# Attention with squared relu and a mixture of experts on one core: blank list entries written in order, first expert tiles gathered sooner, V's parts ahead of the scores

## The chip, the core and the metric

The kernel runs on one core of a Trainium2 chip. The metric is device microseconds of one execution; a kernel's time is the median of its runs. The engines are TensorE (PE, with its weight loads PEld), VectorE (DVE), ScalarE (ACT), GpSimd (POOL) and SyncE (SP), which only issues copies. Lines such as L143 are lines of the kernel before.

## The reference

Eight batches of 2496 tokens go through attention with squared relu instead of a softmax, and the result is gated by u. Every token then goes to the one expert of eight that its logits choose.

```python
scores = (1.0 / S) * np.matmul(z, z.transpose(0, 2, 1))     # z: 8 x 2496 x 64
x = u * np.matmul(np.maximum(scores, 0.0) ** 2, v)          # u, v: 8 x 2496 x 256

logits = x @ w_gate                                         # 19968 tokens, 8 experts
expert_idx = np.argmax(logits, axis=1)
probs = softmax(logits)                                     # gate_w: the chosen one's
for e in range(E):
    xe = x[expert_idx == e]
    out[expert_idx == e] = gate_w * (np.maximum(xe @ w1[e], 0.0) @ w2[e])   # 256 x 1024, 1024 x 256
```

## The kernel before

**Numbers in two parts.** Products are made in float32r with each operand split into a high part, a cast (`hi`, `xh`, `vt[:, 0]`), and a low part, the rest (`lo`, `xl`, `vt[:, 1]`). The cast is mostly ACT's work, the subtraction DVE's or POOL's.

**Attention.** Queries are taken in five chunks (`c`, 512 wide, the last 448), keys in ten pairs of 128 (`kp`), so there are 8 x 5 x 10 = 400 steps (`steps`, the last is `LAST` = 399, `NKP` = 10). In a step, `weighted` (L325 to L328) multiplies V's pair by the scores of this step, 12 matmuls, and `scores` runs three steps ahead (`LA` = 3): four matmuls (L299, L300), a relu out of PSUM (L301), a square (L302) and a cast (L304) on ACT, the low part (L306) on DVE. Scores are symmetric: a block above the diagonal is transposed on DVE (`turn`, L267), written to DRAM (L270) and reloaded for a later chunk (`bring`, L277), where it needs only a cast (L291) and a subtraction (L292). At the end of a chunk `gate_x` multiplies the sum by u on DVE (L350). z, u and V are loaded by SP (L121, L151, L138), V into a ring of four raw blocks; `split_v` casts a V pair on ACT (L143) and subtracts on DVE or, from the third pair of the first batch, on POOL (L145).

**Routing.** For each chunk `turn_rows` writes x's rows to DRAM (`xrows`, L370) and `route` computes the expert of each token, its gate and its place; `place` scatters a 64-byte entry (gate, token number) per token to `lst` (L445, POOL). Each expert has a region of `lst`, big enough for all tokens. Places that no token takes must hold a blank entry (token number past the end), so `blank` (L233) writes blank entries over the places that a batch may reach, half a batch per call: 104 x 8 x 192 values, 624 KB. The calls for batch 0 and the tails of the regions stand in `constants`, on POOL; those for batch b + 1 stand at the sixth and ninth step of chunk 1 of batch b, on SP.

**Experts.** After batch 6 a first list (`A`) of tiles of 512 tokens is made from the regions that are already full, so that six tiles can run while the rest is still routed; after batch 7 a second list (`F`). For a tile, POOL loads its entries (`load_e`, L659), gathers its token rows (`load_x`, L670) and the expert's weights (`load_w`, L644, two halves of 1 MB each); `turn_x` transposes the rows on DVE (L700), writes them to DRAM (L703) and reloads them (L705); `split_x` casts them (L715, ACT) and subtracts (L716, DVE); `up` and `down` multiply (L733, L754, L756); `finish` scatters the rows to the output (L767). The work ahead of the first tile is put at steps counted from the last one (`loads`).

**What sets the order.** A scheduler orders the instructions of each engine's queue by priority and by its own simulated time, so an instruction with nothing to wait for may be moved well ahead of its place in the program. Within `pinned`, an instruction is kept behind the last one of its engine that stands ahead in the program. `declare_no_dep` tells the scheduler that two accesses of the same tensor don't touch the same places, so neither waits for the other. Each engine, SP too, issues in order.

Of the kernel before, what the change touches and what calls it, by code (L numbers as in the profile page):

```python
# [19 lines left out]
P = 128  # L20
# [3 lines left out]
E = 8  # L24
F = 1024
QC = 512
ENT, PAD = 16, 12
BIG, SMALL = 512, 256
# [20 lines left out]
def fused_kernel(ctx: ExitStack, tc: tile.TileContext, zt, ut, v, wg, wcat, out):  # L49
    nc = tc.nc  # L50
    B, _, SP = zt.shape
    S = SP - KQ
    NK = SP // P
    NKP = NK // 2
    NTOK = B * S
    chunks = [(q, min(QC, S - q)) for q in range(0, S, QC)]
    NC_ = len(chunks)
# [148 lines left out]
    def constants():  # L206
        nc.vector.memset(wg2.bitcast(F32), 0.0)
        nc.vector.tensor_copy(wg2[:, :, 0:E], wg_sb)
        nc.vector.tensor_tensor(wg2[:, :, E:2 * E], wg_sb, wg2[:, :, 0:E].bitcast(F32), op=ALU.subtract)
        for ti, tf in iotas:  # L210
            nc.vector.tensor_copy(tf, ti)
        nc.vector.tensor_copy(base, base0)

        nc.vector.memset(padrow, 0.0)
        nc.gpsimd.dma_start(xrows[NTOK:NTOK + 1, :], padrow)
        nc.gpsimd.memset(pad, 0.0)
        nc.gpsimd.iota(pad.bitcast(I32)[:, 1:PAD * ENT:ENT], pattern=[[0, PAD]], base=NTOK, channel_multiplier=0)
        blank(0, 0, nc.gpsimd)
        blank(0, 1, nc.gpsimd)
        w = BIG * ENT // P  # L220
        nc.gpsimd.dma_start(regions[:, NTOK * ENT:].rearrange("e (p k) -> p e k", k=w),
                            pad[:, 0:w].unsqueeze(1).broadcast_to([P, E, w]))
        nc.gpsimd.dma_start(lst[NROW * SMALL:].rearrange("(p r) k -> p (r k)", p=P), pad[:, 0:w])

    regions = lst[0:E * CAP].rearrange("(e c) k -> e (c k)", e=E)
    blanks, scatters = [], []

    def blank(b, h, eng=None):

        w, n = PAD * ENT, S // PAD // 2  # L230
        assert n * PAD * 2 == S and n <= P
        at = (b * S + h * S // 2) * ENT
        i = (eng or nc.sync).dma_start(regions[:, at:at + n * w].rearrange("e (p k) -> p e k", k=w),  # L233
                                       pad[0:n].unsqueeze(1).broadcast_to([n, E, w]))
        for _, o in scatters:
            tc.declare_no_dep(i.ins, o.ins, reason="places of another batch")
        blanks.append((b, i))
# [153 lines left out]
    def route(t0, n, ns, lw, gw):  # L391
# [28 lines left out]
        def place():  # L420
# [22 lines left out]
            for j in range(ns):  # L443
                m = min(P, n - j * P)
                i = nc.gpsimd.indirect_dma_start(  # L445
                    out=lst, out_offset=bass.IndirectOffsetOnAxis(ap=posi[:m, j:j + 1], axis=0),
                    in_=gw[:m, j, :], in_offset=None)
                for _, o in scatters:
                    tc.declare_no_dep(i.ins, o.ins, reason="places are distinct")
                for of, o in blanks:  # L450
                    if of > t0 // S:
                        tc.declare_no_dep(i.ins, o.ins, reason="places of another batch")
                scatters.append((t0 // S, i))

        return [choose, exps, place]
# [194 lines left out]
    def load_e(i):  # L650
        which, t, k = order[i]
        en = ents[i] = sb.tile([P, BS, ENT], F32, name="ent", bufs=6)
        to = en.rearrange("p s w -> p (s w)")
        eidx = lists[which]["eidx"]
        parts = [(by4, t, 0, BS)] if k == BS else [(by2, t, 0, 2)]
        if k == 3:
            parts.append((lst, eidx.shape[1] - N3 + t - 2 * ND - NB, 2, 3))
        for src, at, a, z in parts:
            nc.gpsimd.indirect_dma_start(out=to[:, a * ENT:z * ENT], out_offset=None, in_=src,  # L659
                                         in_offset=bass.IndirectOffsetOnAxis(ap=eidx[:, at:at + 1], axis=0))  # L660

    def token(i, s):
        return bass.IndirectOffsetOnAxis(ap=ents[i].bitcast(I32)[:, s, 1:2], axis=0)
# [154 lines left out]
    def at(s, work):  # L818
        todo.setdefault(s, []).append(work)

    for b in range(B):
        for c in range(NC_):
            s0 = (b * NC_ + c) * NKP
            at(s0 + 2, lambda b=b, c=c: fetch_u(b, c))
            if c == 1 and b + 1 < B:
                for h in range(2):
                    at(s0 + 5 + 3 * h, lambda b=b, h=h: blank(b + 1, h))
            if b == 0:
                continue
            f, z = {0: (-NKP * 4 + 1, 4), 1: (-NKP * 4 + 1, 4), 2: (-NKP * 4 + 1, 4), 3: (-NKP * 5 + 4, 7), 4: (-NKP * 4, 3)}[c]  # L830
# [2 lines left out]
        for kp in range(NKP):  # L833
            if b:
# [8 lines left out]
    ready[2] = scores(*steps[2])  # L843
    bg.append(constants)
    later = []
    loads = {NKP + 4: [lambda: load_e(0)],
             NKP + 3: [lambda: load_e(1)],
             NKP + 2: [lambda: load_x(0)],
             NKP + 1: [lambda: load_w(0, 0)],
             NKP - 1: [lambda: load_w(0, 1)],  # L850
             NKP - 3: [lambda: load_w(1, 0)],
             NKP - 4: [lambda: load_x(1)],
             NKP - 5: [lambda: turn_x(0), lambda: load_e(2)],
             1: [lambda: load_x(2), lambda: load_e(3)],
             0: [lambda: turn_x(1)]}
    for q in range(LP + 1):
# [1 line left out]
    for s, (b, c, kp) in enumerate(steps):  # L858
# [7 lines left out]
                fetch_v(0, kp + 2)  # L866
        for key in plan.get(s, []):
            bring(*key)
        if s + LA <= LAST:
            ready[s + LA] = scores(*steps[s + LA])  # L870
        if s < NKP:
            if kp + 1 < NKP:
                pinned(lambda: split_v(0, kp + 1))
            if kp % 2 == 0 and kp // 2 + 2 < NC_:
                pinned(lambda: split_z(0, kp // 2 + 2))
        if s == LAST - 1:
            pinned(lambda: split_x(0))
        weighted(b, c, kp, j == 0, j == NKP - 1, *ready.pop(s), accs[b, c])
# [118 lines left out]
```

## Time and profile before

| | us |
|---|---|
| median of 3 runs | 2303.61 |
| lowest, highest | 2300.22, 2307.38 |
| the profiled execution | 2306.15 |
| its span, first to last instruction | 2304.4 |
| PE busy in the span | 2233.8 (97%) |
| DVE, ACT, POOL busy | 1653.1 (72%), 1368.1 (59%), 673.9 (29%) |
| mean granted clock of PE, 1 is full speed | 0.989 |

The profile is of one execution. Attention takes some 1364 us of the span, the experts the rest. Busy PE is time in which matmuls run; the ends of matmuls are modelled, and at half clock the same matmul counts as longer. The idle time in front of an instruction is put down to what released it. Full clock is 2.4 GHz, half is 1.2.

### The profile page before, as it was taken

Reading aid. Unit: us, or ns where it says so; the run is one execution under the profiler, and the core shown is the slowest. Engines: PE = TensorE matmul, PEld = TensorE weight load, DVE = VectorE, ACT = ScalarE, POOL = GpSimd, SP = SyncE. Lnnn points to the kernel's source line nnn. Section 1 sums busy time; section 2 is a strip of 40 time slices with the busy share of each in tenths; the row PEclk is TensorE's granted clock in tenths of the full one; section 3 lists DMA queues with packets and bytes.
Section 4 is the critical chain, followed back from the end, with each engine's and each line's share of the span. In section 5 each row is a group of like instructions: output and inputs, shape, how many; then the busy total and the mean of one; then the engine's idle time right before and its main releaser. Section 6 shows DMA issues by size and latency. Waiting matters only on the chain. (4 is left out here: it accounts for less than half of the span.)

```text
span 2304.4 us, 31091 instructions
## 1 busy us (share of the span) xinstructions
PE 2233.8 (97%) x10864; PEld 1864.5 (81%) x10864; DVE 1653.1 (72%) x2798; ACT 1368.1 (59%) x1818; POOL 673.9 (29%) x724
## 2 busy tenths in 40 slices
PE   5999999999999999999999989999999999999997
PEld 3788788788888888887887878888888888888886
DVE  5687887887887888878878767566566675666653
ACT  4667757857768658667667643454454454554543
POOL 2210020120120120210220344545445555545521
PEclk8999999999999999999999999999999999999999
DMA  8865774775666756657657674555465556556520
GB/s 263 248 183 146 220 191 138 221 178 172 202 162 181 222 141 195 194 142 230 178 129 215 188 225 140 193 166 183 136 200 187 185 186 193 180 164 223 180 87 22
DMA packets 247180, 414.28 MB, mean 180 GB/s; under 512 B 105539, under 2 KB 146056, under 8 KB 227558
## 3 DMA queue, kind: packets, MB, share of 16 engines
q1 hardware_dynamic: 214006, 291.08, 44.1%
q0 software_dynamic: 33008, 121.12, 16.5%
q8 instruction: 87, 1.43, 0.3%
q14 instruction: 79, 0.65, 0.1%
HBM read 254.55 MB, written 158.07 MB: 179 GB/s over the span
## 5 line engine op out<-in xcount | busy, mean ns | idle before, releaser
L325 PE MATMUL acc<-thi,t 128*128 128x512 f32 (+1 forms) x1200 | 453.8, 389 | 23.8 <-ACT t L143 21.2
L328 PE MATMUL acc<-thi,t 128*128 128x512 f32 (+1 forms) x1200 | 462.3, 388 | 0.9 <-POOL t L145 0.5
L445 POOL DMA_INDIRECT lst<-gw,posi x160 | 172.6, 1078 | 963.9 <-DVE posi L442 468.0
L327 PE MATMUL acc<-tlo,t 128*128 128x512 f32 (+1 forms) x1144 | 444.4, 389 | 0.9 <-DVE tlo L306 0.5
L737 ACT ACTIVATE t<-ph 128x512 fp32r<-128x512 f32 (+1 forms) x328 | 192.5, 588 | 342.2 <-PE ph L733 262.0
L733 PE MATMUL ph<-thi,t 128*128 128x512 f32 (+2 forms) x1248 | 377.8, 362 | 14.7 <-ACT thi L715 9.2
L738 DVE SCALAR_TENSOR_TENSOR t<-ph,t 128x512 fp32r<-128x512 f32 (+1 forms) x328 | 220.5, 674 | 229.8 <-ACT t L737 190.6
L754 PE MATMUL y<-t,t 128*128 128x512 f32 x1062 | 379.3, 397 | 1.7 <-DVE tf L765 1.4
L301 ACT ACTIVATE tf<-ps_s 128x1024 f32<-128x1024 f32 (+1 forms) x240 | 242.2, 1017 | 231.5 <-PE ps_s L300 224.5
L756 PE MATMUL y<-t,t 128*128 128x256 f32 x1062 | 290.0, 281 | 2.3 <-DVE t L738 2.3
L325 PEld LDWEIGHTS acc<-thi,t 128*128 128x128 f32 x1200 | 226.3, 189 | 71.3 <-ACT t L143 24.0
L733 PEld LDWEIGHTS ph<-thi,t 128*128 128x128 f32 x1248 | 226.4, 190 | 52.5 <-ACT thi L715 9.3
L328 PEld LDWEIGHTS acc<-thi,t 128*128 128x128 f32 x1200 | 226.8, 189 | 43.9 <-POOL t L145 1.9
L302 ACT ACTIVATE tf<-tf 128x1024 f32<-128x1024 f32 (+1 forms) x240 | 250.4, 1053 | 4.6
L327 PEld LDWEIGHTS acc<-tlo,t 128*128 128x128 f32 x1144 | 216.7, 189 | 42.9 <-DVE tlo L306 3.5
L306 DVE TENSOR_TENSOR tlo<-tf,thi 128x1024 fp32r<-128x1024 f32 (+1 forms) x168 | 203.6, 1215 | 62.0 <-ACT thi L304 59.4
L754 PEld LDWEIGHTS y<-t,t 128*128 128x128 f32 x1062 | 198.0, 188 | 44.7 <-DVE tf L765 1.8
L267 DVE STREAM_TRANSPOSE s<-tf 128x1024 f32<-128x1024 f32 x160 | 197.5, 1235 | 47.1 <-ACT tf L302 42.7
L733 PE MATMUL ph<-tlo,t 128*128 128x512 f32 (+2 forms) x624 | 225.7, 362 | 2.2 <-issue 1.5
L767 POOL DMA_INDIRECT out_dram<-tf,ent x160 | 165.6, 1035 | 184.5 <-DVE tf L765 125.0
L756 PEld LDWEIGHTS y<-t,t 128*128 128x128 f32 x1062 | 200.5, 189 | 14.8 <-DVE t L738 3.7
L670 POOL DMA_INDIRECT rows<-xrows,ent x160 | 164.5, 1028 | 107.5 <-DMA ent<-lst,lfeidx 64.9
(238 smaller groups left out, 3962.7 us busy)
## 6 DMA issues: line engine op xcount, KB each, us to landing
scr<-s SPq DMA_DIRECT2D x80, 1024.0 KB
s<-scr SPq DMA_DIRECT2D x320, 256.0 KB
vr<-in_v_dram SPq DMA_DIRECT2D x80, 256.0 KB
u<-in_ut_dram SPq DMA_DIRECT2D x32, 512.0 KB
xrows<-th SPq DMA_DIRECT2D x128, 128.0 KB
far<-th SPq DMA_DIRECT2D x31, 512.0 KB
th<-far SPq DMA_DIRECT2D x124, 128.0 KB
zr<-in_zt_dram SPq DMA_DIRECT2D x36, 256.0 KB
```

Of the source, the lines that this page charges most:

```text
L267: nc.vector.transpose(out=to, in_=a.rearrange("p i (t s k) -> p i t s k", t=4, s=G))
L301: nc.scalar.activation(a[:, :, :n], ps[:, :, :n], AF.Relu)
L302: nc.scalar.activation(a[:, :, :n], a[:, :, :n], AF.Square)
L306: nc.vector.tensor_tensor(lo[:, :, :n], a[:, :, :n], hi[:, :, :n].bitcast(F32), op=ALU.subtract)
L325: nc.tensor.matmul(acc[d][:, :n], lhsT=vh, rhs=hi[:, i, :n], start=first and i == 0, stop=False)
L327: nc.tensor.matmul(acc[d][:, :n], lhsT=vh, rhs=lo[:, i, :n], start=False, stop=False)
L328: nc.tensor.matmul(acc[d][:, :n], lhsT=vl, rhs=hi[:, i, :n], start=False, stop=last and i == 1)
L733: nc.tensor.matmul(o, lhsT=w1[:, part, dd, fs], rhs=xx[:, dd, :n], start=p == 0, stop=p == 5)
L737: nc.scalar.activation(hh[:, :m], ph[:, :m], AF.Relu)
L738: nc.vector.scalar_tensor_tensor(hl[:, :m], ph[:, :m], 0.0, hh[:, :m].bitcast(F32), op0=ALU.max, op1=ALU.subtract)
L754: nc.tensor.matmul(y, lhsT=hh[:, cs], rhs=w2[:, f % 2].rearrange("p i d -> p (i d)"), start=f == 0, stop=False)
L756: nc.tensor.matmul(y[:, 0:D], lhsT=hl[:, cs], rhs=w2[:, f % 2, 0, :], start=False, stop=f == NF - 1)
```

## The change

It has three parts. First, the blanks: those of batch 0 and the tails move from POOL to SP and from `constants` to steps 6, 7 and 8, and every blank is now pinned to its place. Second, the first expert tiles: entries, rows and the transpose of the first tiles stand at earlier steps, the weights at the same ones, and the entry loads of list `A` and the scatters of the last batch are declared to have no dependence on each other. Third, in the first chunk of the first batch `split_v` for the next step stands ahead of `scores` in a step instead of behind.

```diff
-        blank(0, 0, nc.gpsimd)
-        blank(0, 1, nc.gpsimd)
+    def tails():
         w = BIG * ENT // P
-        nc.gpsimd.dma_start(regions[:, NTOK * ENT:].rearrange("e (p k) -> p e k", k=w),
-                            pad[:, 0:w].unsqueeze(1).broadcast_to([P, E, w]))
-        nc.gpsimd.dma_start(lst[NROW * SMALL:].rearrange("(p r) k -> p (r k)", p=P), pad[:, 0:w])
+        nc.sync.dma_start(regions[:, NTOK * ENT:].rearrange("e (p k) -> p e k", k=w),
+                          pad[:, 0:w].unsqueeze(1).broadcast_to([P, E, w]))
+        nc.sync.dma_start(lst[NROW * SMALL:].rearrange("(p r) k -> p (r k)", p=P), pad[:, 0:w])
...
-        i = (eng or nc.sync).dma_start(regions[:, at:at + n * w].rearrange("e (p k) -> p e k", k=w),
+        i = nc.sync.dma_start(regions[:, at:at + n * w].rearrange("e (p k) -> p e k", k=w),
...
+                for o in firsts:
+                    tc.declare_no_dep(i.ins, o.ins, reason="places of an earlier batch")
                 scatters.append((t0 // S, i))
...
-            nc.gpsimd.indirect_dma_start(out=to[:, a * ENT:z * ENT], out_offset=None, in_=src,
-                                         in_offset=bass.IndirectOffsetOnAxis(ap=eidx[:, at:at + 1], axis=0))
+            d = nc.gpsimd.indirect_dma_start(out=to[:, a * ENT:z * ENT], out_offset=None, in_=src,
+                                             in_offset=bass.IndirectOffsetOnAxis(ap=eidx[:, at:at + 1], axis=0))
+            if which == "A":
+                firsts.append(d)
+                for of, o in scatters:
+                    if of == B - 1:
+                        tc.declare_no_dep(d.ins, o.ins, reason="places of a later batch")
...
+    for h in range(2):
+        at(6 + h, lambda h=h: pinned(lambda: blank(0, h)))
+    at(8, lambda: pinned(tails))
...
-                    at(s0 + 5 + 3 * h, lambda b=b, h=h: blank(b + 1, h))
+                    at(s0 + 5 + 3 * h, lambda b=b, h=h: pinned(lambda: blank(b + 1, h)))
...
-    loads = {NKP + 4: [lambda: load_e(0)],
-             NKP + 3: [lambda: load_e(1)],
-             NKP + 2: [lambda: load_x(0)],
+    loads = {2 * NKP - 2: [lambda: load_e(0)],
+             2 * NKP - 3: [lambda: load_e(1)],
+             NKP + 4: [lambda: load_x(0)],
+             NKP + 3: [lambda: load_e(2)],
              NKP + 1: [lambda: load_w(0, 0)],
+             NKP: [lambda: load_x(1)],
              NKP - 1: [lambda: load_w(0, 1)],
              NKP - 3: [lambda: load_w(1, 0)],
-             NKP - 4: [lambda: load_x(1)],
-             NKP - 5: [lambda: turn_x(0), lambda: load_e(2)],
+             NKP - 2: [lambda: turn_x(0)],
              1: [lambda: load_x(2), lambda: load_e(3)],
              0: [lambda: turn_x(1)]}
...
+        if s < NKP and kp + 1 < NKP:
+            pinned(lambda: split_v(0, kp + 1))
         if s + LA <= LAST:
             ready[s + LA] = scores(*steps[s + LA])
-        if s < NKP:
-            if kp + 1 < NKP:
-                pinned(lambda: split_v(0, kp + 1))
-            if kp % 2 == 0 and kp // 2 + 2 < NC_:
-                pinned(lambda: split_z(0, kp // 2 + 2))
+        if s < NKP and kp % 2 == 0 and kp // 2 + 2 < NC_:
+            pinned(lambda: split_z(0, kp // 2 + 2))
```

## Rows read from the trace of the kernel before

**Rows 1.** The page, parts 1 and 2: PE's busy time, granted clock by slice.

```profile
PE 2233.8 (97%) x10864; PEld 1864.5 (81%) x10864; DVE 1653.1 (72%) x2798; ACT 1368.1 (59%) x1818; POOL 673.9 (29%) x724
...
PEclk8999999999999999999999999999999999999999
```

**Rows 2.** Stretches: span, busy (count) PE PEld DVE ACT POOL, clock, DMA share, GB/s.

```profile
40.00:60.00 20.00, 6.34 (x13) 4.14 (x14) 5.19 (x5) 2.31 (x4) 2.63 (x2) 0.60 0.92 297
...
59.40:64.60 5.20, 5.09 (x12) 4.03 (x13) 0.68 (x1) 0.06 (x1) 1.82 (x2) 0.50 1.01 413
...
540.00:800.00 260.00, 258.57 (x1177) 211.48 (x1177) 215.52 (x345) 184.62 (x199) 31.66 (x43) 1.00 0.68 195
...
1340.00:1380.00 40.00, 30.80 (x142) 26.52 (x141) 26.07 (x48) 18.72 (x26) 18.00 (x18) 0.87 0.71 225
...
1373.10:1378.80 5.70, 5.56 (x13) 4.16 (x14) 1.92 (x2) 0.69 (x2) 2.14 (x3) 0.51 0.41 105
```

**Rows 3.** PE's waits, whole run: line, releaser: us in total, times, longest.

```profile
PE acc L325 <- ACT t L143: 21.2, 5, 12.7
...
PE ph L733 <- ACT thi L715: 9.2, 1, 9.2
```

**Rows 4.** PE's waits between 100 and 1340 us, the whole list.

```profile
PE ps_s L299 <- ACT tf L301: 4.0, 6, 1.1
```

**Rows 5.** Timeline of DVE: start, us, operation; last gates of chunks.

```profile
210.97 1.15 DVE L350 SCALAR_TENSOR_TENSOR x<-acc,u 128x448 f32<-128x448 f32 x2
...
1202.11 1.14 DVE L350 SCALAR_TENSOR_TENSOR x<-acc,u 128x448 f32<-128x448 f32 x2
...
1336.99 1.28 DVE L350 SCALAR_TENSOR_TENSOR x<-acc,u 128x512 f32<-128x512 f32 x2
...
1363.55 1.16 DVE L350 SCALAR_TENSOR_TENSOR x<-acc,u 128x448 f32<-128x448 f32 x2 [0.28 <-PE acc L328]
```

**Rows 6.** Timeline of SP, first 60 us.

```profile
6.18 0.33 SPq L138 DMA_DIRECT2D vr<-in_v_dram  x1
...
8.96 38.51 SPq L233 DMA_DIRECT2D lst<-pad  x14
...
49.67 1.55 SPq L138 DMA_DIRECT2D vr<-in_v_dram  x1
```

**Rows 7.** Timeline of all engines, first 60 us, with idle time before.

```profile
12.87 0.79 PE L325 MATMUL acc<-thi,t 128*128 128x512 f32 x2 [2.52 <-ACT thi L304]
...
19.18 0.50 PE L325 MATMUL acc<-thi,t 128*128 128x512 f32 x1 [1.25 <-ACT t L143]
...
58.84 0.62 ACT L143 CAST t<-vr 128x512 fp32r<-128x512 f32 x1 [17.15 <-DMA vr<-in_v_dram]
...
59.51 0.80 PE L325 MATMUL acc<-thi,t 128*128 128x512 f32 x1 [12.68 <-ACT t L143]
```

**Rows 8.** Groups of ACT, 0 to 100 us: busy, mean ns, idle before.

```profile
L302 ACT ACTIVATE tf<-tf 128x1024 f32<-128x1024 f32 x17 | 17.6, 1059 | 0.1
...
L301 ACT ACTIVATE tf<-ps_s 128x1024 f32<-128x1024 f32 x17 | 17.0, 1023 | 20.7 <-PE ps_s L300 17.5 <-DVE tlo L306 2.6 <-DVE tlo L310 0.7
...
L304 ACT CAST thi<-tf 128x1024 fp32r<-128x1024 f32 x11 | 11.4, 1049 | 1.4 <-PE acc L328 1.3
...
L143 ACT CAST t<-vr 128x512 fp32r<-128x512 f32 x10 | 6.1, 619 | 17.2 <-DMA vr<-in_v_dram 17.1
```

**Rows 9.** Timeline of all engines at the passage to the experts.

```profile
1351.12 1.20 DVE L700 STREAM_TRANSPOSE th<-rows 128x1024 f32<-128x1024 f32 x1
...
1361.21 0.81 SPq L705 DMA_DIRECT2D th<-far  x2
...
1372.14 1.04 ACT L715 CAST thi<-th 128x1024 fp32r<-128x1024 f32 x1 [5.69 <-DMA th<-far]
...
1373.24 1.22 PE L733 MATMUL ph<-thi,t 128*128 128x512 f32 x2 [9.20 <-ACT thi L715]
```

**Rows 10.** The blank's line: duration ns min, median, max of SP's issues.

```profile
L233 SPq DMA_DIRECT2D lst<-pad x14: 386/2189/8157, 9.0 to 45.0; - x14
```

More of the change, by code (lines that the diff above doesn't have):

```diff
@@ L217, in constants, with blank @@
         nc.gpsimd.iota(pad.bitcast(I32)[:, 1:PAD * ENT:ENT], pattern=[[0, PAD]], base=NTOK, channel_multiplier=0)
-        blank(0, 0, nc.gpsimd)
-        blank(0, 1, nc.gpsimd)
+    def tails():
         w = BIG * ENT // P
-        nc.gpsimd.dma_start(regions[:, NTOK * ENT:].rearrange("e (p k) -> p e k", k=w),
-                            pad[:, 0:w].unsqueeze(1).broadcast_to([P, E, w]))
-        nc.gpsimd.dma_start(lst[NROW * SMALL:].rearrange("(p r) k -> p (r k)", p=P), pad[:, 0:w])
+        nc.sync.dma_start(regions[:, NTOK * ENT:].rearrange("e (p k) -> p e k", k=w),
+                          pad[:, 0:w].unsqueeze(1).broadcast_to([P, E, w]))
+        nc.sync.dma_start(lst[NROW * SMALL:].rearrange("(p r) k -> p (r k)", p=P), pad[:, 0:w])
     regions = lst[0:E * CAP].rearrange("(e c) k -> e (c k)", e=E)
-    blanks, scatters = [], []
-    def blank(b, h, eng=None):
+    blanks, scatters, firsts = [], [], []
+    def blank(b, h):
         w, n = PAD * ENT, S // PAD // 2
```

## Prediction

> **What bounds the kernel now.** I first read the page's busy shares: TensorE (PE) is busy for 97% of the span, so the time is PE's work plus PE's gaps [rows 1]. The line of granted clock over 40 slices says where to look: it leaves full speed in the first slice only, and the stretches show more closely that the second place is the passage from attention to the experts [rows 1, 2]. From 40 to 60 us PE is busy 6.34 of 20 us at clock 0.60, from 1340 to 1380 us 30.8 of 40 at 0.87, while 540 to 800 us, a stretch in the middle of attention, loses 1.4 of 260 us [rows 2]. PE's waits over the whole run give the causes: 21.2 us in five waits for ACT's cast of a V block (the high part), and 9.2 us in one for the cast of the first expert tile [rows 3]. Between 100 and 1340 us PE's list of waits holds one entry, 4.0 us for PSUM, and nothing that ends on a DMA [rows 4]. So there are two places to win at, and a long stretch in which there is almost nothing to win and something to lose.
>
> **How much the first place holds.** The gate of a batch's last chunk on VectorE (DVE) marks the end of the batch: 210.97 us for the first batch and 1202.11 us for the seventh, so six batches take 991.1 us, 165.2 each [rows 5]. The first batch therefore costs 210.97 - 165.2 = 45.8 us more than a later one. Of that, 12.87 us pass before the first weighted matmul [rows 7], less the one block of scores that is ahead of its usual place by then (4 matmuls; at full clock one takes 258.57 us / 1177 = 0.22 us of PE [rows 2], so 0.9 us). The rest, 45.8 - 12.9 + 0.9 = 33.8 us, is what stalls and half clock cost: 21.2 us waits for V casts, the rest smaller waits and matmuls that come at half clock behind the stalls, 5.2 us / 12 = 0.43 us each instead of 0.22 [rows 2, 3].
>
> **Part 1, the blanks leave the start.** The scheduler pulled all 14 later halves of blank entries to the front: SP writes them in one row, 8.96 to 47.47 us [rows 6]. V's sixth block could only be requested behind them, at 49.67 us (the one before it went out at 6.18 us) [rows 6]; ACT waited 17.15 us for it and PE 12.68 [rows 7]. With each write bound to its place on SP's queue this wait goes: 12.7 us, and with it the half clock behind it: 12 matmuls in 59.4 to 64.6 us at clock 0.50 [rows 2], 5.2 - 12 x 0.22 = 2.6 us more. The V requests still wait for a buffer (four raw blocks), which a cast frees; casts come earlier by part 2. Two halves and the tails (624 KB each; 288 KB together) now stand on SP at steps 6, 7 and 8, ahead of the requests for the last V blocks and what the scheduler puts behind. A half held SP between 0.39 us (nothing in the way) and 8.16 us [rows 10], 38.51 / 14 = 2.75 us on the mean: about 2 x 2.75 + 1.3 = 6.8 us of SP, spread over three steps of 3.75 us (below), against a V request that goes out two to three steps ahead. I take it as hidden; without that cover it costs up to 6.8 us once. POOL loses four issues, off the path.
>
> **Part 2, V's parts ahead of the scores.** The other four waits make 21.2 - 12.7 = 8.5 us. The first of them shows the pattern: the first weighted block was through, and PE stood 1.25 us before the second, for a V cast that had to pass the relu, the square and the cast of a later score block on ACT [rows 7]. Those three take 1.02 + 1.06 + 1.05 = 3.1 us, and the V cast 0.62 [rows 8]. Ahead of them, each V cast ends 3.1 us earlier; single waits of that kind go, longer ones lose 3.1 us, and with the chain that they start (a late weighted block, late scores, a late relu) more. Nothing is added: the score block gives way by 0.62 us, and it is used three steps later. What is late next is ACT itself: in this chunk it has 3.1 + 0.62 = 3.75 us a step against PE's 16 x 0.22 = 3.5, a bound by 2.5 us over ten steps. DVE and POOL have one V half and the transposes beside it, and the transfers are near full: the stretch from 40 to 60 us stood at 0.92 of the DMA engines, and even without the 14 blanks the first batch's copies must then run closer together.
>
> Of 33.8 us I take 27.5 as won and leave 6.3 for ACT as the bound (2.5 us, above) and for V blocks and operations that come later than planned while the transfers are crowded, an estimate of 3.8 us from the smaller waits that make up the rest of the 33.8. The ends: 33.8 if all goes, 15.3 if only the blanks' wait and its half clock go (12.7 + 2.6).
>
> A rule of the Trainium skill speaks against moving the first two halves from POOL to SP: "DMA: Bandwidth & Descriptors", section "Queues, rings and completion order", has each engine take turns between queue rows but serve one row's ring in order, and SP has one row. By it a V request behind a blank waits for the whole blank, where POOL's row would have shared. The row of SP shows the in-order half of it, 17.15 us for the one block behind 14 writes [rows 6, 7]; the sharing half no run here shows. By the rule the first term would lose the 6.8 us named above, by the row's slack nothing.
>
> **Part 3, the later blanks in the middle.** Fourteen halves go to chunk 1 of the first seven batches, 14 x 2.75 = 38.5 us of transfer at the crowded rate. In the middle the DMA share is 0.68 and no PE wait ends on a DMA [rows 2, 4]. Queued behind each on SP are reloads of kept scores, u and z blocks. Cost: 0 to 2.75 us each, 0 to 38.5; nearest is the row of PE's waits, so I take 2 us, and 8 as a serious end. A gain is excluded, for nothing is taken away there. The first scatter comes long after its blank, so it gains no wait.
>
> **Part 4, the first expert tiles.** The first tile's rows were gathered early; its transpose on DVE ran at 1351.12 us, its reload through DRAM was asked for at 1361.21, and ACT cast it at 1372.14, a chain of 21.0 us; PE then started after 9.20 us [rows 9]. The change puts that transpose three steps earlier, from the sixth-last to the ninth-last; the weight gathers keep their steps. The last chunk lies between two gates, 1336.99 and 1363.55 us [rows 5], 2.66 us a step, so the transpose comes 8.0 us earlier, at 1343.1, and a chain of the same length ends 8.0 us earlier: PE waits 1.2 of the 9.2 us. The half clock behind the stall goes too: 13 matmuls in 1373.1 to 1378.8 us at clock 0.51 [rows 2], 5.7 - 13 x 0.22 = 2.8 us. Gain 8.0 + 2.8 = 10.8. If the trip through DRAM is quicker, as it then stands before the last weight gathers, 12.0; if the transpose keeps its place in DVE's queue, 0. Dropping the wait of the third entry load for the last batch's scatters frees POOL, and gathers sooner what might crowd the trip; at nothing.
>
> **The sum.** 27.5 + 10.8 - 2 = 36.3 us. The profiled execution took 2306.15 us, its span 2304.4; 2306.15 - 36.3 = 2269.9. The median of the three runs, 2303.61, is 2.5 us below the profiled one, so 2267.3, rounded 2267.
>
> **Rivals.** (a) The first chunk becomes bound by transfers or by ACT: only the blanks' own wait and its half clock go, 15.3 us; 15.3 + 10.8 - 2 = 24.1, 2279.5. For it: 0.92 DMA share, ACT level with PE. Against: the same chunk of later batches, with the same score blocks, lies in the stretch without DMA waits [rows 4]. Chance 0.17. (b) The passage keeps its stall, the transposed tile crowded by 1 MB weight gathers that now start sooner: 27.5 - 2 = 25.5, 2278. Chance 0.10. (c) The change doesn't do what it says: the order that the scheduler finds still has blanks or scores ahead of the V blocks in the first chunk, about 10 us of it won, with the passage 10.8 and the middle's 2 lost: 2285. Chance 0.06. (d) Slower: the blanks in the middle. Each holds SP 2.75 us and the engines as long again, so a kept-score reload behind it comes 5.5 us late; if PE had to wait for each, 14 x 5.5 = 77 us, 2303.6 - 38.3 + 77 = 2342. It decides from 38.3 / 14 = 2.7 us a blank. For it: SP's line is served in order [rows 6]. Against: no wait for a reload shows on PE in 1240 us [rows 4]. Chance 0.04.
>
> **Chances and range.** The forecast, 2256 to 2276, has 0.60, rivals (a) to (c) 0.33, (d) 0.04, the rest 0.03 for a chain in the first chunk that I don't see. Its low end is both upper ends together, 33.8 + 12.0 = 45.8 us, 2258, less 2 for the spread of the runs; the range reaches up over (a) to (c) to 2287. About 0.3%, 6.9 us, is what a measurement here can tell from no change: faster than that 0.91, within it 0.05, slower 0.04.
>
> **What would show it.** Right: SP's blanks stand in pairs about 165 us apart; the first batch's last gate comes near 183 us; PE's waits for V casts fall from 21.2 to under 6 us; the wait for the first tile's cast is under 2 us and the clock stays full there. Wrong: the last gate of the first batch after 195 us (parts 1 and 2), a wait of over 4 us for the tile (part 4), batches of more than 166 us (part 3), or new gaps in the expert stage, which I hold to move as a whole.

## The result, and the profile after

The changed kernel takes 2269.47 us (median of 6 runs, 2266.32 to 2272.0), the kernel before 2302.84 us on the same chip (6 runs, 2299.68 to 2307.38): a ratio of 0.9854, 95% interval 0.984 to 0.9869, or 33.4 us. The forecast was 2267 us, in a range of 2256 to 2287. The profiled execution of the changed kernel took 2266.60 us, 2.9 us under its median, and the one of before stood some 3 us over its own; so the pair of profiles differs by 39.5 us, and about 6 us of that are scatter.

Some helpers stand one to eight lines further down in the changed kernel: the weighted matmuls are L326, L328 and L329, the scores L300 and L301, their relu, square, cast and low part L302, L303, L305 and L307, V's cast L143 as before, the gate L351, the blanks L234, the first tile's transpose L708 and its cast L723. The split of a part of z is a cast on POOL (L128) and one on DVE (L131) with the low parts on DVE (L132, L133). In the kernels with z early or its request alone, the lines of the attention stand two further down again.

The page, parts 1 and 2, answering [rows 1]:

```profile
PE 2223.7 (98%) x10864; PEld 1859.5 (82%) x10864; DVE 1653.5 (73%) x2798; ACT 1368.8 (60%) x1818; POOL 672.1 (30%) x720
...
PEclk9999999999999999999999999999999999999999
```

PE's busy time falls by 10.1 us for the same 10864 matmuls: fewer of them ran at half clock. The rest of the gain is idle time. Stretches of the changed kernel, answering [rows 2] (span; busy time and count of PE, PEld, DVE, ACT, POOL; clock, DMA share, GB/s):

```profile
0.00:20.00 20.00, 14.52 (x49) 8.31 (x50) 11.86 (x16) 15.61 (x18) 4.49 (x25) 1.00 0.46 158
20.00:40.00 20.00, 14.22 (x53) 10.21 (x51) 12.27 (x23) 9.53 (x11) 5.48 (x5) 0.91 0.85 254
40.00:60.00 20.00, 16.51 (x57) 12.21 (x58) 14.93 (x13) 12.70 (x16) 7.68 (x5) 0.83 0.69 213
60.00:80.00 20.00, 20.00 (x89) 16.18 (x88) 19.05 (x20) 16.53 (x19) 2.19 (x1) 1.00 0.80 241
...
540.00:800.00 260.00, 258.57 (x1185) 211.32 (x1184) 212.90 (x359) 181.38 (x196) 36.35 (x49) 1.00 0.71 202
...
1340.00:1380.00 40.00, 40.00 (x207) 33.46 (x206) 34.25 (x120) 15.89 (x29) 17.44 (x17) 1.00 0.60 185
```

The passage (last line) runs at full clock with no gap, and the middle has the same 258.57 us of PE as before. The first chunk is better but not mended: from 20 to 60 us PE ran 110 matmuls where two stretches like 60 to 80 us would hold 178. These 68, at 0.22 us, are 15 us.

The last gates of the batches on DVE give the stages; here the first, the seventh and the eighth of the changed kernel, answering [rows 5] (start, duration, engine, line):

```profile
191.72 1.15 DVE L351 SCALAR_TENSOR_TENSOR x<-acc,u 128x448 f32<-128x448 f32 x2
...
1182.90 1.14 DVE L351 SCALAR_TENSOR_TENSOR x<-acc,u 128x448 f32<-128x448 f32 x2
...
1344.56 1.16 DVE L351 SCALAR_TENSOR_TENSOR x<-acc,u 128x448 f32<-128x448 f32 x2 [0.52 <-PE acc L329]
```

| stage | before, us | after, us | gain | forecast |
|---|---|---|---|---|
| start to the first batch's last gate | 210.97 | 191.72 | 19.25 | 27.5 |
| six batches, to the seventh's gate | 991.14 | 991.18 | 0.0 | -2 |
| eighth batch | 161.44 | 161.66 | -0.2 | 0 |
| its gate to the fourth expert tile's cast | 76.19 | 61.70 | 14.5 | 10.8 |
| from there to the last instruction | 864.66 | 858.64 | 6.0 | 0 |

The first four make 33.5 us, against a forecast of 36.3 and medians that differ by 33.4. The last row is taken as scatter: the stretch took 857.6 us in the kernel with V's split alone, which has the old expert tiles, and 860.3 in the kernel with the new ones alone (both below). The total was right by two errors of size that partly cancel, so in part by luck.

PE's waits from 0 to 100 us in the changed kernel (what waited, for what; us in total, times, longest), answering [rows 3]:

```profile
PE acc L326 <- ACT t L143: 8.3, 4, 4.5
PE acc L326 <- ACT thi L305: 2.1, 1, 2.1
PE ps_s L300 <- DVE t L133: 1.3, 2, 0.9
```

The 12.7 us wait is gone, and the waits for V's casts fall from 21.2 to 8.3 us, two of which are long (2.56 and 4.46 us). The wait for the first expert tile has no entry any more.

### The profile page after: what moved, and what is told of

Its sections match the earlier page's. It is cut to its first block, busy times and chain, and to the rows that moved or that the text cites. A ratio compares the mean times of both kernels' runs of the same rounds, so it can differ in the third digit from the quotient of the medians.

```text
span 2264.9 us, 31096 instructions
## 1 busy us (share of the span) xinstructions
PE 2223.7 (98%) x10864; PEld 1859.5 (82%) x10864; DVE 1653.5 (73%) x2798; ACT 1368.8 (60%) x1818; POOL 672.1 (30%) x720
## 4 chain that ended last, share of the span: by engine, by line
PE 83%; issue 7%; DMA 3%; POOL 3%; DVE 2%; ACT 2%; SPq 0%; POOLq 0%; DVEq 0%; ACTq 0%
PE acc L329 15%; PE acc L326 15%; PE ph L741 14%; PE acc L328 14%; PE y L762 10%; PE y L764 5%; PE ps_s L300 4%; PE ps_s L301 4%; PE pt L378 2%; POOL rows L678 1%; POOL out_dram L775 1%; DMA scr<-s 1%; DMA out_dram<-tf,ent 1%; DMA rows<-xrows,ent 1%; DMA ent<-lst,lfeidx 1%
## 5 line engine op out<-in xcount | busy, mean ns | idle before, releaser
L329 PE MATMUL acc<-thi,t 128*128 128x512 f32 (+1 forms) x1200 | 460.6, 386 | 0.9 <-POOL t L145 0.8
L326 PE MATMUL acc<-thi,t 128*128 128x512 f32 (+1 forms) x1200 | 450.8, 387 | 7.0 <-ACT t L143 4.9
L328 PE MATMUL acc<-tlo,t 128*128 128x512 f32 (+1 forms) x1144 | 442.1, 387 | 0.9 <-DVE tlo L307 0.5
L302 ACT ACTIVATE tf<-ps_s 128x1024 f32<-128x1024 f32 (+1 forms) x240 | 242.4, 1018 | 227.9 <-PE ps_s L301 225.2
L326 PEld LDWEIGHTS acc<-thi,t 128*128 128x128 f32 x1200 | 225.4, 188 | 51.8 <-ACT t L143 5.8
L329 PEld LDWEIGHTS acc<-thi,t 128*128 128x128 f32 x1200 | 225.6, 188 | 43.2 <-POOL t L145 1.7
L303 ACT ACTIVATE tf<-tf 128x1024 f32<-128x1024 f32 (+1 forms) x240 | 250.4, 1053 | 4.6
L328 PEld LDWEIGHTS acc<-tlo,t 128*128 128x128 f32 x1144 | 215.3, 188 | 42.3 <-DVE tlo L307 3.1
L307 DVE TENSOR_TENSOR tlo<-tf,thi 128x1024 fp32r<-128x1024 f32 (+1 forms) x168 | 203.0, 1212 | 61.2 <-ACT thi L305 58.8
```

The costliest lines, as they stand in the source:

```text
L302: nc.scalar.activation(a[:, :, :n], ps[:, :, :n], AF.Relu)
L303: nc.scalar.activation(a[:, :, :n], a[:, :, :n], AF.Square)
L307: nc.vector.tensor_tensor(lo[:, :, :n], a[:, :, :n], hi[:, :, :n].bitcast(F32), op=ALU.subtract)
L326: nc.tensor.matmul(acc[d][:, :n], lhsT=vh, rhs=hi[:, i, :n], start=first and i == 0, stop=False)
L328: nc.tensor.matmul(acc[d][:, :n], lhsT=vh, rhs=lo[:, i, :n], start=False, stop=False)
L329: nc.tensor.matmul(acc[d][:, :n], lhsT=vl, rhs=hi[:, i, :n], start=False, stop=last and i == 1)
```

## Experiments

Each kernel was run beside the kernel before on the same chip; ratios are against that. How far two profiles of like code differ is needed first: three profiles with the first chunk of before have the first batch's last gate at 209.78, 210.97 and 213.58 us, and four with that of the changed kernel at 190.12, 191.18, 191.72 and 193.38 us. Differences of less than about 4 us in that gate are not read below.

**One part alone.** The kernel before with only the blanks and tails moved:

```diff
-        blank(0, 0, nc.gpsimd)
-        blank(0, 1, nc.gpsimd)
...
+    for h in range(2):
+        at(6 + h, lambda h=h: pinned(lambda: blank(0, h)))
+    at(8, lambda: pinned(tails))
...
-                    at(s0 + 5 + 3 * h, lambda b=b, h=h: blank(b + 1, h))
+                    at(s0 + 5 + 3 * h, lambda b=b, h=h: pinned(lambda: blank(b + 1, h)))
```

> The kernel before with the blanks' part of the change alone (those of batch 0 and the tails on SP at steps 6 to 8, all pinned); V's casts stay behind the scores, the first expert tiles at their old steps. Theory: the wait for V's sixth block (12.7 us) and the half clock behind it (2.6 us) go and nothing else, so the first batch's last gate comes at about 211.0 - 15.3 = 195.7 us and the time is about 2288 us; later batches stay at 165.2 us; the wait for the first tile's cast stays near 9 us. Rival 1: the V casts alone made the gain and the blanks were only in front of a late cast: the gate stays after 205 us and the time near 2300. Rival 2: the blanks cost in the middle: batches above 166 us.

2283.95 against 2300.72 us, ratio 0.9919 (0.9905 to 0.9933), 16.8 us. The first gate came at 196.37 us, 14.6 earlier: the step of the prediction that valued the blanks' wait with its half clock at 15.3 us holds by itself. V's casts still cost PE 8.2 us in four waits, longest 4.5, nearly as in the changed kernel. Against the expectation, the first tile's cast was waited for 3.4 us and not 9, beside 3.8 us for DVE in the last chunk; more on this below.

The kernel before with only V's split ahead of the scores:

```diff
+        if s < NKP and kp + 1 < NKP:
+            pinned(lambda: split_v(0, kp + 1))
         if s + LA <= LAST:
             ready[s + LA] = scores(*steps[s + LA])
-        if s < NKP:
-            if kp + 1 < NKP:
-                pinned(lambda: split_v(0, kp + 1))
```

> The kernel before with V's cast ahead of the scores in the first chunk alone; the blanks stay at the front of SP's queue. Theory: the long wait behind the blanks stays at some 12 us, of the other waits (8.5 us) and their half clock about 4 us go, as the changed kernel's first batch ended 19.3 us earlier and the blanks account for 15.3: gate at about 207 us, time about 2299 us. Rival: the casts' place decides and the blanks' wait shrinks as well, because a buffer for the sixth block comes free before the blanks are reached: gate before 198 us, time below 2292.

2291.85 us, ratio 0.996 (0.9947 to 0.9973), 8.9 us. The gate came at 203.06 us, 7.9 earlier, more than expected; the block behind the 14 blanks is still waited for, 17.2 us. Beside the blanks' part it is worth less: from 196.37 to 191.72 us, 4.7. The two parts take some of the same waits.

The kernel before with only the expert tiles' part (the steps and the declared independence):

```diff
-    loads = {NKP + 4: [lambda: load_e(0)],
-             NKP + 3: [lambda: load_e(1)],
-             NKP + 2: [lambda: load_x(0)],
+    loads = {2 * NKP - 2: [lambda: load_e(0)],
+             2 * NKP - 3: [lambda: load_e(1)],
+             NKP + 4: [lambda: load_x(0)],
+             NKP + 3: [lambda: load_e(2)],
...
-             NKP - 5: [lambda: turn_x(0), lambda: load_e(2)],
+             NKP - 2: [lambda: turn_x(0)],
```

> The kernel before with the part for the first expert tiles alone (steps and the declared independence). Theory: the gate of the last chunk stays at 1363.6 us, the wait for the first tile's cast (9.2 us) and the half clock behind it go, and by the third expert tile the run is 15 us ahead of the kernel before, as in the changed kernel; time about 2288 us. If the 5.5 us that the changed kernel's profile gained later in the expert stage belong to this part, about 2282; if they are the scatter of single runs, they are not seen in the times. Rival: the early turn only pays because the rest of the changed kernel shifted the load: a wait of over 4 us stays and the time is above 2294.

2288.72 us, ratio 0.9949 (0.9936 to 0.9961), 12.0 us, near the 2288 expected if the gain later in the expert stage is scatter; the gate of the first batch stays (209.78), and the wait for the tile is gone. The three parts alone make 16.8 + 8.9 + 12.0 = 37.7 us, together 33.4.

**What holds the first chunk: V's cast, or z's split?** In the changed kernel the longest wait, 4.46 us, is put down to V's cast. My first theory was that this cast is still late. So V was split two steps ahead instead of one:

```diff
     ready[1] = scores(*steps[1])
+    split_v(0, 1)
     ready[2] = scores(*steps[2])
...
-        if s < NKP and kp + 1 < NKP:
-            pinned(lambda: split_v(0, kp + 1))
+        if s < NKP and kp + 2 < NKP:
+            pinned(lambda: split_v(0, kp + 2))
```

> The changed kernel with V's cast one more step ahead in the first chunk (the pair after next, and the second pair before the third score block). Theory: what is left in the first chunk of the changed kernel (8.3 us of waits for V's casts, 4.5 of them in one) is a cast pinned behind the cast of a score block that PE multiplies only after the weighted block before it; one step more frees it, so these waits fall below 3 us, the first batch's last gate comes 8 to 12 us earlier than 191.7 us (at 180 to 184), and the time is about 2260 us. Rival 1: ACT is the bound in this chunk, so the wait moves to the score blocks' casts and the gate moves by under 3 us, time 2267 to 2270. Rival 2: V's raw blocks come too late for it, and ACT waits for a transfer in front of its scores: gate later than 191.7 us.

2273.3 us, ratio 0.9881 (0.9865 to 0.9897), and the gate at 195.89: no gain. That the gate came later was the sign of rival 2, but ACT's waits in the first 100 us hold none for a V block. The same wait stands there with the same length. PE's line in that kernel, and ACT's ahead of it:

```profile
43.31 0.76 PE L326 MATMUL acc<-thi,t 128*128 128x512 f32 x2 [4.46 <-ACT t L143]
```

```profile
37.98 1.94 ACT L302 ACTIVATE tf<-ps_s 128x1024 f32<-128x1024 f32 x2 [6.79 <-PE ps_s L301]
39.80 2.00 ACT L303 ACTIVATE tf<-tf 128x1024 f32<-128x1024 f32 x2
41.70 1.04 ACT L305 CAST thi<-tf 128x1024 fp32r<-128x1024 f32 x1
42.63 0.62 ACT L143 CAST t<-vr 128x512 fp32r<-128x512 f32 x1
```

ACT was not late, it was idle for 6.79 us. What came late was the pair of score blocks from PE; relu, square and cast of the score block end at 42.74 us, so even a V cast at no time could have let PE start only 0.57 us sooner. The theory that V's cast alone is late falls. The changed kernel has the same chain on ACT, and its timelines show what the scores stood behind (POOL, DVE, PE and ACT, in this order):

```profile
29.15 1.61 POOL L128 CAST t<-s 64x512 fp32r<-64x512 f32 x1
...
32.31 1.23 DVE L307 TENSOR_TENSOR tlo<-tf,thi 128x1024 fp32r<-128x1024 f32 x1
33.45 0.68 DVE L132 TENSOR_TENSOR t<-s,t 64x512 fp32r<-64x512 f32 x1
34.16 0.69 DVE L133 TENSOR_TENSOR t<-s,t 64x512 fp32r<-64x512 f32 x1
...
35.28 0.39 PE L300 MATMUL ps_s<-t,t 128*128 128x512 f32 x1
...
36.39 1.94 ACT L302 ACTIVATE tf<-ps_s 128x1024 f32<-128x1024 f32 x2 [6.03 <-PE ps_s L301]
38.22 2.00 ACT L303 ACTIVATE tf<-tf 128x1024 f32<-128x1024 f32 x2
40.11 1.04 ACT L305 CAST thi<-tf 128x1024 fp32r<-128x1024 f32 x1
41.04 0.62 ACT L143 CAST t<-vr 128x512 fp32r<-128x512 f32 x1
...
41.72 0.50 PE L326 MATMUL acc<-thi,t 128*128 128x512 f32 x1 [4.46 <-ACT t L143]
```

Read upwards: PE waits for ACT, ACT for the scores, and the scores start right behind the split of z's next part, whose last half ends on DVE at 34.85 us. That split is pinned behind the scores of the step before, by a line that the change left as it was. Two things are not as simple as the chain. PE had no gap in front of these scores: it ran the weighted block ahead of them until 35.28 us, so it is their place in PE's order that is late, and the trace doesn't show that the scheduler gave them this place because of the split. And the weighted block that waits at 41.72 us had its own scores by 33.54, when their low part ended (L307); it stood only for its V cast, which ACT had in line behind the relu, the squares and the first cast of the later pair. The kernel with V two steps ahead freed that cast, and the wait went to the next weighted block, whose scores are late themselves. The second theory: it is the place of z's split that keeps the pair of score blocks late. The test asks for z's last two parts at the start and splits each one pair of blocks earlier, ahead of the scores:

```diff
     fetch_z(0, 2)
+    fetch_z(0, 3)
+    fetch_z(0, 4)
...
+    split_z(0, 2)
     ready[2] = scores(*steps[2])
...
+        if s < NKP and kp % 2 == 0 and kp // 2 + 3 < NC_:
+            pinned(lambda: split_z(0, kp // 2 + 3))
         if s + LA <= LAST:
             ready[s + LA] = scores(*steps[s + LA])
-        if s < NKP and kp % 2 == 0 and kp // 2 + 2 < NC_:
-            pinned(lambda: split_z(0, kp // 2 + 2))
```

> The changed kernel with z's tiles loaded at once and split one pair of steps earlier in the first chunk (the third tile before the third score block, then the tile three ahead instead of two). Theory after the run with V two steps ahead: what PE waits for is not the V cast but the score block before it, whose matmuls can't start before z's tile is split on POOL and DVE (in the changed kernel the z split ends at 34.8 us, the scores start at 35.3, their five ACT operations end at 41.1, PE stands 4.5 us); with z split earlier the scores stand two steps ahead again, the 4.5 us wait goes, the first batch's last gate comes at 183 to 187 us instead of 191.7, and the time is about 2263 us. Rival: three engines are full in this chunk (ACT 3.75 us a step), so the wait moves to casts or low parts and the gate stays within 2 us of 191.7, time 2268 to 2271.

2254.69 us (2252.32 to 2255.02) against 2298.54, ratio 0.9809 (0.9793 to 0.9824): below both kernels. The pair of score blocks that stood at 35.28 us, the first batch's last gate, and the stretches with z early:

```profile
19.90 0.47 PE L302 MATMUL ps_s<-t,t 128*128 128x512 f32 x1
...
177.95 1.15 DVE L353 SCALAR_TENSOR_TENSOR x<-acc,u 128x448 f32<-128x448 f32 x2
```

```profile
20.00:40.00 20.00, 17.12 (x74) 13.28 (x74) 19.88 (x27) 16.19 (x21) 10.51 (x8) 1.00 0.93 293
40.00:60.00 20.00, 20.00 (x90) 16.55 (x89) 15.88 (x16) 17.26 (x19) 5.30 (x3) 1.00 0.99 299
```

The gate is 210.97 - 177.95 = 33.0 us before that of the kernel before, and no wait for a V cast is left. PE is busy all through 40 to 60 us at full clock with ACT at 17.26 of 20 us and the DMA engines at 0.99: neither ACT nor the transfers hold PE there. The fullest engine from 20 to 40 us is DVE, busy for 19.88 of 20.

This kernel moves z's request and z's split at once. The request alone, with the splits at their old place:

```diff
     fetch_z(0, 2)
+    fetch_z(0, 3)
+    fetch_z(0, 4)
...
-            if kp % 2 == 0 and kp // 2 + 3 < NC_:
-                fetch_z(0, kp // 2 + 3)
```

> The changed kernel with z's fourth and fifth parts requested at the start, as in the kernel with z early, but with z's splits at their old place behind the scores. Theory A, the place of the split in the order of the engines is what holds the pair of score blocks: the wait of about 4.5 us near 42 us stays, the first batch's last gate comes near 191.7 us (190 to 194), as in the changed kernel, and the time near 2269 us. Theory B, z's data came late, and the early request is what won the 13.8 us: the gate comes before 182 us and the time is under 2261 us.

2267.23 us, ratio 0.9869 (0.9852 to 0.9885), the gate at 190.87, and the wait is there again:

```profile
42.20 0.80 PE L328 MATMUL acc<-thi,t 128*128 128x512 f32 x1 [4.46 <-ACT t L143]
```

Nothing was won. This test moved less than it meant to, for the scheduler had the requests early already: in the changed kernel SP asks for the fourth part of z at 3.62 us and for the last as below, and their splits begin at 29.15 and 42.81 us:

```profile
5.05 0.47 SPq L121 DMA_DIRECT2D zr<-in_zt_dram  x1
```

So z's data were early in both kernels, and this kernel differs from the one with z early only in the place of the splits: it is that place which moves the gate, from 190.87 to 177.95 us.

Two more kernels ask what V's place is worth once z is early: V behind the scores again, and V two steps ahead.

```diff
-        if s < NKP and kp + 1 < NKP:
-            pinned(lambda: split_v(0, kp + 1))
         if s < NKP and kp % 2 == 0 and kp // 2 + 3 < NC_:
             pinned(lambda: split_z(0, kp // 2 + 3))
         if s + LA <= LAST:
             ready[s + LA] = scores(*steps[s + LA])
+        if s < NKP and kp + 1 < NKP:
+            pinned(lambda: split_v(0, kp + 1))
```

> The kernel of the run with z split earlier, with V's casts behind the scores again, as in the kernel before. Theory: V's place matters by itself, about what it gave beside the blanks in the changed kernel (4.7 us in the first batch's last gate, 196.4 against 191.7): gate at about 182 to 184 us against 178.0, time about 2259 us. Rival: once scores stand two steps ahead, a V cast behind one block more has enough lead and its place is worth nothing: gate at 178 to 179.5 us, time 2254 to 2256.

2258.69 us, ratio 0.9803 (0.9789 to 0.9816), gate 181.72, just short of what the theory expected.

```diff
+    split_v(0, 1)
     ready[2] = scores(*steps[2])
...
-        if s < NKP and kp + 1 < NKP:
-            pinned(lambda: split_v(0, kp + 1))
+        if s < NKP and kp + 2 < NKP:
+            pinned(lambda: split_v(0, kp + 2))
```

> The kernel of the run with z split earlier, with V's cast one more step ahead. Theory: nothing on PE waits for a V cast any more, so the gate stays within 1.5 us of 178.0 or comes later by the 0.8 us by which the second V cast delays the first weighted block; time 2254 to 2257. Rival: the low parts of V on POOL are what is left (1.2 us wait), and the gate comes 1.5 us or more earlier.

2259.12 us, ratio 0.9812 (0.9796 to 0.9828), gate 180.77; a wait of 4.2 us for a low part on DVE has come instead. The three ratios with z early, 0.9809, 0.9803 and 0.9812, can't be told apart, and the gates, 177.95, 181.72 and 180.77, lie within the scatter: with z early, V's place is worth too little to be measured here.

**The passage: the steps, or the declared independence?** The change moves the steps of the entry loads, gathers and transpose, and also frees the entry loads of the first tiles from the last batch's scatters. The changed kernel without the second:

```diff
-            if which == "A":
-                firsts.append(d)
-                for of, o in scatters:
-                    if of == B - 1:
-                        tc.declare_no_dep(d.ins, o.ins, reason="places of a later batch")
```

> The changed kernel without the declared independence of the first list's entry loads and the last batch's scatters; the earlier steps stay. In the changed kernel the first tile's transpose ran 41.5 us before the last gate, in the kernel before 12.4 us; the steps alone are worth 8 us of that. Theory A: the independence does most of it, because the entry loads else queue on POOL behind the last batch's scatters; here the transpose runs 15 to 25 us before the gate, and the wait for the first tile's cast is 0 to 3 us; time within 4 us of the changed kernel. Theory B: the steps do it; the transpose stays at about 41 us before the gate and the time is that of the changed kernel.

2268.14 us, ratio 0.9873 (0.9855 to 0.9891), no wait for the tile; its transpose runs 39 us before the gate. And the changed kernel with the old steps (the first lines of the list of loads put back):

```diff
-    loads = {2 * NKP - 2: [lambda: load_e(0)],
-             2 * NKP - 3: [lambda: load_e(1)],
-             NKP + 4: [lambda: load_x(0)],
-             NKP + 3: [lambda: load_e(2)],
+    loads = {NKP + 4: [lambda: load_e(0)],
+             NKP + 3: [lambda: load_e(1)],
+             NKP + 2: [lambda: load_x(0)],
...
-             NKP - 2: [lambda: turn_x(0)],
+             NKP - 5: [lambda: turn_x(0), lambda: load_e(2)],
```

> The changed kernel with the old steps for the first expert tiles; the declared independence stays. Theory A: the transpose runs some 30 us before the gate, no wait of over 1 us is left for the first tile and the time is that of the changed kernel within 2 us. Theory B: the transpose is back at about 12 us before the gate, the wait near 9 us, and the time about 12 us above the changed kernel, 2281.

2277.24 us, ratio 0.9908 (0.9894 to 0.9922): on the same chip 9.1 us above the kernel with the new steps alone (2268.14). The tile is waited for again (PE's waits from 1300 us to the end):

```profile
PE ph L741 <- DVE t L746: 5.2, 3, 4.3
PE ph L741 <- ACT thi L723: 5.1, 1, 5.1
```

The steps do it; of the independence nothing can be measured.

**The later blanks.** The changed kernel with each of the 14 later halves written four times (the same blanks to the same places, so nothing else changes):

```diff
-                    at(s0 + 5 + 3 * h, lambda b=b, h=h: pinned(lambda: blank(b + 1, h)))
+                    for _ in range(4):
+                        at(s0 + 5 + 3 * h, lambda b=b, h=h: pinned(lambda: blank(b + 1, h)))
```

> The changed kernel with each of the fourteen later blank halves written four times at its place: 42 more copies of 624 KB. Theory: they lie in the slack of SP and of the transfers (share 0.65 to 0.7), so the batches stay at 165.2 us and the time rises by less than 4 us. Rival: each blank that SP issues delays the reloads behind it by what it takes, 2.75 us at the crowded rate; four in a row by 11 us, so PE waits and the time rises by 20 to 115 us.

2269.31 us, ratio 0.987 (0.985 to 0.9889). The stretch in the middle, to be held against that of the changed kernel above:

```profile
540.00:800.00 260.00, 258.56 (x1184) 211.33 (x1183) 212.81 (x357) 182.95 (x197) 36.08 (x47) 1.00 0.80 225
```

The DMA share goes from 0.71 to 0.80 and PE's busy time stays at 258.56 us. The six batches take 991.16 us, against 991.18 in the changed kernel. 42 more copies of 624 KB cost nothing that can be seen, so the 14 of the change cost nothing either.

**How steady is the passage?** The kernel before once more, for a second profile:

> The kernel before once more, for a second profile. Theory: the 6 us that the changed kernel's profile gained in the expert stage beyond the passage are the scatter of single executions in that stage, so here attention takes the same 1363.6 us within 2 us and the experts behind it 930 to 945 us. Rival: 940.9 us is what this stage always takes in the kernel before.

2305.84 us. Attention took 1371.1 us up to its last gate and not 1363.6, against the expectation: the first batch 2.6 us more, the last one 5.0. The experts behind it took 933.0 us, as expected. The stall at the passage took another form (PE's waits from 1300 us to the end):

```profile
PE acc L327 <- DVE s L310: 3.6, 1, 3.6
PE ph L733 <- ACT thi L715: 3.4, 1, 3.4
```

Two waits of 3.6 and 3.4 us stand where [rows 3] has one of 9.2, and the first of them lies in the last chunk; the kernel with the blanks alone has the same pair. From the seventh batch's gate to the end, the four profiles of kernels with neither the new steps nor the independence took 1091.2, 1097.0, 1099.4 and 1102.3 us, the nine with the new steps 1082.0 to 1087.2. So the part is worth about 14 us by these means (1097.5 and 1083.7), 12.0 by the medians of the runs with it alone (9 to 15 by the interval of their ratio). The four spread over 11 us and the nine over 5; the two of the kernel before lie 2.9 us apart, so how much of the spread is one execution against another and how much one kernel against another isn't shown.

## Why the prediction was right in sum, and where a step failed

**The ceiling: right.** 33.8 us from the comparison of the first batch with the later ones; with z early, 33.0 of them were reached.

**Part 1, the blanks: right.** 15.3 us for the wait and its half clock; alone the part moved the gate by 14.6 us. Its cover held too: SP's line in the changed kernel shows a blank of the first batch right behind a V request, and the tails behind it:

```profile
43.94 0.35 SPq L138 DMA_DIRECT2D vr<-in_v_dram  x1
44.34 0.48 SPq L234 DMA_DIRECT2D lst<-pad  x1
44.87 0.49 SPq L222 DMA_DIRECT2D lst<-pad  x1
45.40 2.82 SPq L224 DMA_DIRECT2D lst<-pad  x1
```

The blank held SP for 0.48 us and not 2.75, the second half, at 56.71 us, for 0.40, and only the tails for longer, 3.3: 4.2 us in all instead of 6.8. ACT's waits in the first 100 us of the changed kernel hold none for a V block. The 6.8 us that the rule of the Trainium skill on rows served in order ("DMA: Bandwidth & Descriptors", section "Queues, rings and completion order") would have charged are not to be seen. How a V request fares with more in the row ahead of it, the changed kernel doesn't show.

**Part 2, V ahead of the scores: the step that failed.** It said that what is late next is ACT itself, by 2.5 us, and left 6.3 of the 33.8 us. 14.5 were left. The row that I read [rows 7] named ACT's V cast, behind relu, square and cast of a later block, and I took the order on ACT as the whole cause. In the long waits ACT stood idle before that chain, for 6.03 us in the changed kernel; what was late were the scores, and in the program they stood behind z's split. Splitting V earlier still won nothing; splitting z earlier moved the gate by 13.8 us. The sign stood in the rows: of ACT's 20.7 us of idle time before the relu, 17.5 ended on PE's scores [rows 8], which doesn't fit an ACT that is late. The kernel before has the same chain ahead of its own long wait (ACT, then PE):

```profile
35.47 1.94 ACT L301 ACTIVATE tf<-ps_s 128x1024 f32<-128x1024 f32 x2 [5.61 <-PE ps_s L300]
...
40.13 0.62 ACT L143 CAST t<-vr 128x512 fp32r<-128x512 f32 x1
...
40.80 0.79 PE L325 MATMUL acc<-thi,t 128*128 128x512 f32 x1 [4.46 <-ACT t L143]
```

The gate of the changed kernel, 191.72 us, lies between the 183 foreseen and the 195 that was to refute parts 1 and 2, and the waits for V's casts, 8.3 us, above the 6 foreseen. Rival (a), bound by transfers or ACT, had 15.3 us for this chunk, nearer the 19.25 than the forecast's 27.5, but for the wrong reason: with z early PE runs from 40 to 60 us without a gap at a DMA share of 0.99.

**Part 3, the blanks in the middle: 0 instead of 2 us.** SP's blanks stand in pairs at 84.00 and 91.58, 251.85 and 256.98 us and so on to 1076.70, 164 to 168 us from pair to pair as foreseen, and hold SP thus (duration ns min, median, max over the whole run, the two halves of batch 0 with them):

```profile
L234 SPq DMA_DIRECT2D lst<-pad x16: 310/411/1287, 44.3 to 1082.0; - x16
```

Rival (d) wanted 2.7 us a blank on the path; neither 14 nor 56 of them showed there.

**Part 4, the passage: right in kind, with the move mis-sized.** 10.8 us forecast, 14.5 in the pair of profiles, 12.0 by the medians, whose interval holds the forecast. The transpose did not move by 8.0 us:

```profile
1303.02 1.20 DVE L708 STREAM_TRANSPOSE th<-rows 128x1024 f32<-128x1024 f32 x1
```

It runs 41.5 us before the gate instead of 12.4, 29 us earlier for three steps in the list. The call is not pinned; with the transpose five steps from the end it ran 12.4 us ahead of the gate in three profiles and 17.4 to 17.5 in the two whose last gate came 5 us later, with eight 39.1 to 41.6 us ahead in nine. Why the scheduler takes it so much further I didn't find out. By the forecast 1.2 us of the wait were to stay; none did. The half clock gave back 3.55 us (2.8 forecast), and 1.7 us of a second wait, for DVE in the up projection, went as well, which I had not counted. Rival (b), weight gathers in the way, did not come about: the first gather went out at 1310.61 us, beside the trip through DRAM, but the tile's cast at 1337.83 waited for no transfer.

**The sum.** 36.3 us forecast, 33.5 by stages. The first chunk gave 8.2 less than foreseen, the passage 3.7 more (1.2 by the medians), the middle 2 more.

## What to carry to other kernels

A wait's named releaser is only the last of a chain: before moving it, look whether its engine was idle ahead of it, and if so go on to what it waited for. Where that engine was busy, its order is the next question, and only an experiment that moves the suspected work answers it. The cost of a stage against its later repetitions gives a ceiling that no list of waits gives, and the part of it that a change leaves is worth another look; here a second move of the same kind was worth 10 to 15 us more. What a copy costs its queue must be taken from the stage into which it is moved, not from the crowded one that it leaves.

## What the runs showed of the hardware that was not expected

The same 624 KB copy held SP for 2.19 us in the median and up to 8.16 us where 14 of them stood in a row [rows 10], and for 0.41 us in the median and up to 1.29 us where they stood one or two at a time (the 16 of the changed kernel). Writing the later ones four times raised the DMA share of the 260 us in the middle from 0.71 to 0.80 and left PE's busy time in it unchanged, to 0.01 us of 258.57.
